# Gated attention in one core: seven block products for the Q projection, as a stage of its own

## The chip, the cores and the metric

The kernel runs on one core of one Trainium2 chip. A core has five engines that run side by side and wait for one another through semaphores: TensorE (matrix products; PE in the profile, and PEld for its weight loads), VectorE (DVE), ScalarE (ACT), GpSimd (POOL) and SyncE (SP), which here only issues transfers. TensorE writes to PSUM, eight banks of 128 x 512 float32; everything else lives in SBUF, and DRAM is reached by DMA. The metric is device time in microseconds. Two runs of the kernel before gave 1958.55 and 1958.67, a median of 1958.61.

## What is computed

The input x has 2048 tokens of 640 features. It is normalized per token, and the result feeds two branches that are multiplied at the end:

```python
def _A_ref(x, k_cache, v_cache, wq, wo):          # 32 heads of 128, last 512 keys of the cache
    q = (x @ wq) split into heads
    scores = einsum("bhqd,bhkd->bhqk", q, k) * DH**-0.5
    p = softmax(scores, axis=-1)
    o = einsum("bhqk,bhkd->bhqd", p, v)
    return o merged over heads @ wo
def _B_ref(x, w1, b1, w2, b2):                    # 640 -> 1728 -> 640
    h = relu(x @ w1 + b1) ** 2
    return h @ w2 + b2
xn = layernorm(x)
out = x + _A_ref(xn, ...) * silu(_B_ref(xn, ...))
```

All data are float32. A product of two float32 matrices is made of three TensorE products: each operand is split into a high part (what TensorE keeps of it) and a low remainder, and high x high, high x low and low x high are summed. So every product of a 128 x 128 block with a 128 x 512 block costs three matmuls of 512 columns, and every operand costs a copy (ScalarE) and a subtraction (VectorE or GpSimd) for its split.

## The kernel before

The tokens form four tiles of 512 (`NTILE`), the 640 features five chunks of 128 (`DC`), the 1728 hidden features of the MLP thirteen chunks and a half one (`FC`), the 512 keys four chunks (`KC`). Heads are worked in pairs (`G` = 2), token tiles in two halves of two.

The first 300 us normalize the tiles and run the MLP of three of the four tiles, with its split weights kept in SBUF; the MLP of the last tile is spread over the beginning and the end of the attention. The split x of each tile goes to DRAM (`xT_d`) and is read back when its half begins.

The attention is a list of 128 units, one for a head and a token tile. For unit i, TensorE forms the scores (`s_mm`, 12 matmuls into four PSUM banks of tag `s`), the value product of the unit before (`v_mm`, 12), the Q projection of the unit after the next (`q_mm`, 15 matmuls with x as the moving operand and wq as weights), and, per pair of units, the output products (`r_mm`, 30). VectorE folds each score bank by a transposing maximum (`max_fold`, tile rdm), ScalarE gathers the folded rows (`gather`), VectorE takes the row maximum (`row`, tile rowm), SyncE stores it to DRAM (m_d) and reads it back as a broadcast over the partitions (bm), and VectorE subtracts it (`shift`, tile e), which frees the score bank. ScalarE takes the exponential (`expo`) and the high part (`p_hi`, tile pt), GpSimd the low part (`p_lo`) and the sum of the halves (`s_add`). The row sums go the same way as the maxima, through s_d and bs, and scale the value product (`o_norm`).

The order is written out by hand: each step is put in a list with a time, `on(when, f, ...)`, relative to its unit's start in a grid of 12.4 us (`PERIOD`), and the list is sorted and issued. The times set the order on every engine's queue; they are not waited for. `load_raw` and `prep` bring and split the weights of the next heads. On SyncE's queue, `row` issues the small store and then the broadcast, which waits for the store to land. `align` puts NOPs between TensorE's instructions so that each unit is 128 of them and stands at the same place in blocks of 256.

Of the kernel before, what the change touches and what calls it, by code (L numbers as in the profile page):

```python
# [8 lines left out]
F32 = mybir.dt.float32  # L9
# [5 lines left out]
P = 128  # L15
# [3 lines left out]
BLOCK = 256  # L19
FIRST_SLOT = 188  # L20
SLOTS = (0, 11, 22, 33, 42)
LEAD_SLOT, LEAD_PADS, LEAD_STEPS = 76, 5, range(19, 23)
# [3 lines left out]
def kernel(  # L26
# [24 lines left out]
    LN_AT = {t: (3, 7) if t == LATE else (5, 9) for t in range(1, NTILE)}  # L51
    SCALE = DH**-0.5
    G = 2
    HALF = 2
    PSUM = bass.MemoryType.PSUM

    cpool = ctx.enter_context(tc.tile_pool(name="const", bufs=1))
    dpool = ctx.enter_context(tc.tile_pool(name="dram", bufs=1, space=bass.MemoryType.DRAM))

# [3 lines left out]
    b1_sb, b2_sb = b_sb[:, :FC], b_sb[:, FC : FC + DC]  # L63
    chunks = [(f0, min(P, F - f0)) for f0 in range(0, F, P)]
# [4 lines left out]
    class Ordered:  # L69
# [16 lines left out]
    xT_d = [  # L86
        [dpool.tile([P, DC, NT], F32, name=f"xT_d{t}_{i}") for i in range(2)]
        for t in range(NTILE)
    ]
    g_d = [dpool.tile([P, DC, NT], F32, name=f"g_d{t}") for t in range(LATE)]  # L90
    s_d = [dpool.tile([P, DC, NT], F32, name=f"s_d{t}") for t in range(NTILE // 2)]
    h_d = {f: dpool.tile([P, NT], F32, name=f"h_d{f}") for f in range(FC - 4, FC)}
# [4 lines left out]
    def products(ps, pairs, first=True, last=True):  # L97
        n = len(pairs)
        for i, ((ah, al), (bh, bl)) in enumerate(pairs):
            nc.tensor.matmul(ps, ah, bh, start=first and i == 0, stop=False)  # L100
            nc.tensor.matmul(ps, ah, bl, start=False, stop=False)  # L101
            nc.tensor.matmul(ps, al, bh, start=False, stop=last and i == n - 1)  # L102

    psx = ctx.enter_context(tc.tile_pool(name="psx", bufs=1, space=PSUM))

    FO, FA = FC - 3, FC - 4
    keep = ctx.enter_context(tc.tile_pool(name="keep", bufs=1))
    mctx, wctx, hctx = ExitStack(), ExitStack(), ExitStack()
    wpa = wctx.enter_context(tc.tile_pool(name="mwa", bufs=1, side="right"))
    wpb = mctx.enter_context(tc.tile_pool(name="mwb", bufs=1))  # L110
    xp = mctx.enter_context(tc.tile_pool(name="mx", bufs=2))
    hp = mctx.enter_context(tc.tile_pool(name="mh", bufs=2))
    ps_h = hctx.enter_context(tc.tile_pool(name="ps_h", bufs=2, space=PSUM, side="right"))
    ps_y = mctx.enter_context(tc.tile_pool(name="ps_y", bufs=DC, space=PSUM))

    w1s, w2s = [], []
    for f, (f0, n) in enumerate(chunks):
        wp = wpa if f < FO else wpb
        if n < P:
            w1s.append([wp.tile([P, DC, 2 * n], F32R, name=f"w1s{f}")])  # L120
        else:
            if f < FA:
                w1p = [wp.tile([P, DC, n], F32R, name=f"w1s{f}_{i}") for i in range(2)]
            else:
                two = keep.tile([P, 2, D], F32R, tag="ot", name=f"w1s{f}", bufs=4)
                w1p = [two[:, i, :].rearrange("p (c n) -> p c n", n=n) for i in range(2)]
            w1s.append(w1p)
        w2s.append([wp.tile([P, D], F32R, name=f"w2s{f}_{i}") for i in range(2)])

    def pad(pool, nbytes):  # L130
        pool.tile([P, nbytes // 4], F32, name="pad")

    pad(wpa, 480)

    def ln_tile(t, b):
        tag = "stage" if b < 2 else "mr"
        return xp.tile([P, D], F32, tag=tag, name=f"xb{t}_{b}")

    LS = {}

    def ln_load(t):
        mv = xp.tile([P, 4, NB], F32, tag="mv", name=f"mv{t}")[:, :2, :]
        sc = xp.tile([P, 3, NB], F32, tag="sc", name=f"sc{t}")
        xn = []
        for b in range(NB):
            xb = ln_tile(t, b)
            r0 = t * NT + b * P
            nc.sync.dma_start(xb, x[r0 : r0 + P, :])
            xn.append(xb)
        LS[t] = mv, sc, xn  # L150

    def ln_block(t, b):
        mv, sc, xn = LS[t]
        st = xp.tile([P, 2, 6], F32, tag="st", name=f"st{t}_{b}", bufs=4)
        hd = D // 2
        for i in range(2):
            dve.bn_stats(st[:, i, :], xn[b][:, i * hd : (i + 1) * hd])
        dve.bn_aggr(mv[:, :, b], st)

    def ln_var(t):  # L160
        mv, sc, xn = LS[t]
        dve.tensor_scalar(sc[:, 0, :], mv[:, 1, :], EPS, None, op0=ALU.add)
        nc.scalar.activation(sc[:, 1, :], sc[:, 0, :], AF.Sqrt)

    def ln_root(t):
        mv, sc, xn = LS.pop(t)
# [7 lines left out]
        return mv  # L174

    def ln_rows(t, mv):
        pm = psx.tile([P, NT], F32, tag="x", name=f"pmv{t}")
        nc.tensor.transpose(pm[: 2 * NB, :P], mv.rearrange("p a b -> p (a b)"), ident)
        row = xp.tile([2 * NB, P], F32, tag="lr", name=f"lr{t}", bufs=1)
        nc.vector.tensor_copy(row, pm[: 2 * NB, :P])  # L180
        d = dpool.tile([2, NT], F32, name=f"mv_d{t}")
        nc.sync.dma_start(d.rearrange("a (b p) -> (a b) p", p=P), row)
        bc = []
        for i in range(2):
            m = xp.tile([P, D], F32, tag="mr", name=f"mr{t}_{i}")[:, :NT]
            nc.sync.dma_start(m, d[i : i + 1, :].to_broadcast([P, NT]))
            bc.append(m)
        xs = [
            keep.tile([P, DC, NT], F32R, tag="acc", name=f"xT{t}_{i}", bufs=2)
            if t % 2  # L190
            else xp.tile([P, DC, NT], F32R, tag=f"xT{i}", name=f"xT{t}_{i}", bufs=1)
            for i in range(2)
        ]
        return bc, xs

    def ln_chunk(t, bc, xs, c):
        xc = xp.tile([P, D], F32, tag="stage", name=f"xc{t}_{c}")[:, :NT]
        nc.sync.dma_start(xc, xT[c * P : (c + 1) * P, t * NT : (t + 1) * NT])
        dve.tensor_tensor(xc, xc, bc[0], op=ALU.subtract)
        nc.vector.tensor_tensor(xc, xc, bc[1], op=ALU.mult)  # L200
        nc.scalar.activation(xs[0][:, c, :], xc, AF.Copy)
        nc.vector.tensor_tensor(xs[1][:, c, :], xc, raw(xs[0][:, c, :]), op=ALU.subtract)

    PRE, BOTH, BR = {}, {}, []

    def biases():
        pb = psx.tile([P, NT], F32, tag="x", name="pb")
        pe.transpose(pb[:, :P], BR.pop(), ident)
        dve.tensor_copy(b1_sb, pb[:, :FC])
        dve.tensor_copy(b2_sb, pb[:, 32 : 32 + DC])  # L210
        split_lo(0, PRE[0, 1], 1, dve)

    def first_reads(br):
        for k in range(2):
            load_part(0, k, k == 0)
# [6 lines left out]
        for f in (1, 2):  # L222
            for k in range(2):
                load_part(f, k)
        return [PRE[0, k] for k in range(2)]

    def ln_first():
        mv = xp.tile([P, 4, NB], F32, tag="mv", name="mv0")
        sc = xp.tile([P, 3, NB], F32, tag="sc", name="sc0")
# [1013 lines left out]
```

## Time and profile before

| | |
|---|---|
| median of two runs | 1958.61 us |
| span of the profiled execution (its own time beside the span isn't told) | 1956.9 us |
| TensorE busy | 1949.2 us, 8612 matmuls |
| VectorE, ScalarE, GpSimd busy | 1537.3, 1187.6, 1376.7 us |
| moved by DMA | 219.13 MB, mean 112 GB/s |
| TensorE clock granted | 1.0 in all but the last stretch |

The profile is one execution on the chip. Its page has the busy time by engine, the chain of work that ended last, and groups of equal instructions with their mean duration and what ended the idle time before them. From the trace come tables by stretch of time, the instructions in order of time, and for a tile how long its transfers took from issue to landing. A matmul's duration there includes its pipeline; the pitch of a row of matmuls is what counts.

### The profile page before, as it was taken

Reading aid. Unit: us, or ns where it says so; the run is one execution under the profiler, and the core shown is the slowest. Engines: PE = TensorE matmul, PEld = TensorE weight load, DVE = VectorE, ACT = ScalarE, POOL = GpSimd, SP = SyncE. Lnnn points to the kernel's source line nnn. Section 1 sums busy time; section 2 is a strip of 40 time slices with the busy share of each in tenths; the row PEclk is TensorE's granted clock in tenths of the full one; section 3 lists DMA queues with packets and bytes.
Section 4 is the critical chain, followed back from the end, with each engine's and each line's share of the span. In section 5 each row is a group of like instructions: output and inputs, shape, how many; then the busy total and the mean of one; then the engine's idle time right before and its main releaser. Section 6 shows DMA issues by size and latency. Waiting matters only on the chain.

```text
span 1956.9 us, 28182 instructions
## 1 busy us (share of the span) xinstructions
PE 1949.2 (100%) x8612; PEld 1612.5 (82%) x8612; DVE 1537.3 (79%) x2638; ACT 1187.6 (61%) x2040; POOL 1376.7 (70%) x757
## 2 busy tenths in 40 slices
PE   9999999999999999999999999999999999999998
PEld 7888888888888888888888888888888888888887
DVE  6523337788888888888888878888888888888865
ACT  5432336766666666666666676666666666666643
POOL 2121226888888888888888888888888888888841
PEclk9999999999999999999999999999999999999999
DMA  6330454333333332332335434433333333332353
GB/s 189 88 119 28 185 198 130 97 94 92 93 92 93 92 92 92 92 92 93 93 91 179 141 117 109 114 114 114 114 113 114 113 114 114 98 92 92 85 189 118
DMA packets 127892, 219.13 MB, mean 112 GB/s; under 512 B 23452, under 2 KB 38086, under 8 KB 126470
## 3 DMA queue, kind: packets, MB, share of 16 engines
q1 hardware_dynamic: 124742, 202.75, 34.3%
q0 software_dynamic: 2864, 14.42, 1.8%
q8 instruction: 77, 1.26, 0.2%
q14 instruction: 65, 0.53, 0.1%
q10 hardware_dynamic: 144, 0.16, 0.0%
HBM read 193.41 MB, written 23.87 MB: 111 GB/s over the span
## 4 chain that ended last, share of the span: by engine, by line
PE 99%; DVE 0%; DMA 0%; ACT 0%; issue 0%; POOL 0%; POOLq 0%
PE pq L77 22%; PE r L77 22%; PE o L77 18%; PE s L77 18%; PE ph L431 7%; PE ly L77 2%; PE py L101 2%; PE py L100 2%; PE py L102 2%; PE lu L77 2%; PE eu L77 1%; PE ph L398 0%; PE py L454 0%; PE py L453 0%; DMA xb<-in_x_dram 0%; PE px L77 0%
## 5 line engine op out<-in xcount | busy, mean ns | idle before, releaser
L77 POOL TENSOR_TENSOR pt<-e,pt 128x1024 fp32r<-128x1024 f32 x256 | 615.8, 2405 | 113.6 <-ACT pt L77 68.2
L77 PE MATMUL r<-ot,wo 128*128 128x512 f32 x1920 | 496.6, 389 | 0.0
L77 PE MATMUL pq<-ax,wq 128*128 128x512 f32 x1920 | 456.1, 389 | 0.0
L77 PEld LDWEIGHTS pq<-ax,wq 128*128 128x128 f32 x1920 | 360.4, 188 | 75.2 <-DVE q L77 0.4
L77 PEld LDWEIGHTS r<-ot,wo 128*128 128x128 f32 x1920 | 360.5, 188 | 74.8
L77 PE MATMUL o<-pt,wv 128*128 128x512 f32 x1536 | 369.2, 389 | 0.0
L77 PE MATMUL s<-q,wk 128*128 128x512 f32 x1536 | 369.0, 389 | 0.0
L77 DVE TRANSPOSE_TENSOR_REDUCE rdm<-s 128x16 f32<-128x512 f32 x512 | 347.6, 712 | 6.0 <-PE s L77 5.8
L77 ACT ACTIVATE e<-e 128x1024 f32<-128x1024 f32 x256 | 269.8, 1054 | 123.8 <-DVE e L77 80.5
L77 PEld LDWEIGHTS o<-pt,wv 128*128 128x128 f32 x1536 | 288.3, 188 | 60.1 <-POOL pt L77 0.4
L77 PEld LDWEIGHTS s<-q,wk 128*128 128x128 f32 x1536 | 288.4, 188 | 59.8
L77 DVE TENSOR_TENSOR e<-s,bm 128x512 f32<-128x512 f32 x512 | 312.3, 665 | 5.8 <-DMA bm<-m_d 5.4
L77 POOL TENSOR_TENSOR su<-e,e 128x1024 f32<-128x1024 f32 x128 | 309.2, 2415 | 0.0
L77 ACT ACTIVATE pt<-e 128x1024 fp32r<-128x1024 f32 x256 | 271.9, 1062 | 6.9
L77 DVE TENSOR_TENSOR acc<-r,acc 128x512 f32<-128x512 f32 x300 | 203.6, 679 | 12.7 <-PE r L77 12.4
L77 ACT ACTIVATE rdm<-rdm 32x64 f32<-32x64 f32 x384 | 97.7, 254 | 182.1 <-DVE rdm L77 179.0
L77 DVE TRANSPOSE_TENSOR_REDUCE rds<-su 128x32 f32<-128x1024 f32 x128 | 158.4, 1237 | 0.3 <-POOL su L77 0.3
L77 DVE TENSOR_TENSOR ot<-o,ot 128x512 fp32r<-128x512 f32 x128 | 88.5, 692 | 86.1 <-ACT ot L77 86.1
L77 ACT ACTIVATE q<-pq 128x512 fp32r<-128x512 f32 x128 | 76.7, 599 | 113.6 <-PE pq L77 113.6
L431 PE MATMUL ph<-xT,w1s 128*128 128x512 f32 x585 | 139.0, 389 | 0.0
L431 PEld LDWEIGHTS ph<-xT,w1s 128*128 128x128 f32 x585 | 109.7, 188 | 22.8
L77 ACT ACTIVATE rds<-rds 32x32 f32<-32x32 f32 x384 | 89.7, 234 | 60.1 <-DVE rds L77 56.6
(137 smaller groups left out, 1942.3 us busy)
## 6 DMA issues: line engine op xcount, KB each, us to landing
bm<-m_d SPq DMA_DIRECT2D x128, 256.0 KB, 3.2
bs<-s_d SPq DMA_DIRECT2D x128, 256.0 KB, 4.0
qr<-in_wq_dram SPq DMA_DIRECT2D x64, 320.0 KB, 4.5
or<-in_wo_dram SPq DMA_DIRECT2D x64, 320.0 KB, 4.7
kr<-in_kT_dram SPq DMA_DIRECT2D x64, 256.0 KB, 4.3
vr<-in_v_dram SPq DMA_DIRECT2D x64, 256.0 KB, 4.3
xT_d<-xT POOLq DMA_DIRECT2D x6, 1280.0 KB, 7.6
ax<-xT_d SPq DMA_DIRECT2D x4, 1280.0 KB, 11.3
```

The source lines that it names most:

```text
L77: ins = method(*args, **kwargs)
L100: nc.tensor.matmul(ps, ah, bh, start=first and i == 0, stop=False)
L101: nc.tensor.matmul(ps, ah, bl, start=False, stop=False)
L102: nc.tensor.matmul(ps, al, bh, start=False, stop=last and i == n - 1)
L431: nc.tensor.matmul(ph, w1s[f][i][:, c, :], xs[j][:, c, :], start=k == 0, stop=k == len(order) - 1,)
```

## The change

The MLP no longer stands first. The kernel now begins with the layer norm and the whole Q projection of all four token tiles, and writes each split Q (high and low, 512 KB for a head and a tile) to DRAM (`q_d`).

For ten heads of the first two tiles the projection is as before, 15 matmuls per head and tile (`conv_mm`). For the other 22 heads there, and all 32 heads of the last two tiles, two heads and two tiles are taken together. Four of the five feature chunks form a 2 x 2 block product, whose eight block products are replaced by seven on sums and differences of blocks (`WINO`, `s_sum`, `t_sum`), with four accumulating banks a to d and some sums made by ScalarE and VectorE in between; the fifth chunk is added as before. A group of two heads and two tiles takes 54 matmuls in place of 60. While this runs, the MLP's weights are split once and stored in DRAM (`pre_split`, `pre_store`).

Then come the 128 attention units. `q_load` reads Q from DRAM, behind bm on SyncE's queue. Score banks are allocated in pairs, and `max_fold` and `shift` work on two banks at once; `s_add` writes over e. Where the Q products stood, a planner (`spread`) puts pieces of the MLP, of all four tiles, so that each unit has about the same number of matmuls; the pieces' operands (x, h, weights) are read from DRAM, and h is stored there. The square of the MLP's ReLU moves from GpSimd to ScalarE. `align` and its NOPs are gone. The gate and the end of the last tiles are rearranged (`close_1`, `close_2`).

```diff
-    def q_mm(i, cs):
-        hf, g, t, h = units[i]
-        if 0 in cs:
-            QPS[i] = bank(f"pq{i}", 1)
-        ws, xs = WQ[hf, h], XT[hf, t]
-        for c in cs:
-            triple(QPS[i], ...)
+    WINO = (
+        ("a", (0, LOW), (0, LOW), True, True),
+        ("b", (0, HIGH), (0, HIGH), True, False),
+        ("b", (0, LAST), (0, LAST), False, True),
+        ("a", ("S", 2), ("T", 2), False, True),
+        ("c", ("S", 1), ("T", 1), True, True),
+        ("d", ("S", 4), (1, HIGH), True, False),
+        ("a", ("S", 3), ("T", 3), False, True),
+        ("d", (0, LAST), (1, LAST), False, True),
+        ("c", (1, LAST), (1, LAST), False, True),
+        ("a", (1, HIGH), ("T", 4), False, False),
+        ("a", (1, LAST), (0, LAST), False, True),
+    )
...
+    def q_store(key, h, t):
+        sp.dma_start(q_d[h, t], raw(QO.pop(key)))
+    def q_load(i):
+        hf, g, t, h = units[i]
+        q = pools["ep"].tile([P, 2, NT], F32R, tag="q", name=f"q{i}", bufs=AHEAD + 1)
+        sp.dma_start(raw(q), q_d[h, hf * TPH + t])
+        Q[i] = (q[:, 0, :], q[:, 1, :])
...
     def s_mm(i, c):
-        SC[i, c] = pools["psb"].tile([P, NT], F32, tag="s", name=f"s{i}_{c}", bufs=KC)
+        if c % 2 == 0:
+            SC[i, c // 2] = two_banks(f"s{i}_{c // 2}")
...
-    def max_fold(i, c):
+    def max_fold(i, k):
         dve.tensor_reduce(
-            RD[i, "m"][:, :, 0, c],
-            SC[i, c].rearrange("p (i b) -> p b i", i=B32),
+            RD[i, "m"][:, :, 0, 2 * k : 2 * k + 2].rearrange("p b c -> p c b"),
+            SC[i, k].rearrange("p c (i b) -> p c b i", i=B32),
...
-    def shift(i, c):
-        dve.tensor_tensor(E[i, k][:, half, :], SC.pop((i, c)), MB[i], op=ALU.subtract)
+    def shift(i, k):
+        m = MB[i][:, None, :].to_broadcast([P, 2, NT])
+        dve.tensor_tensor(E[i, k], SC.pop((i, k)), m, op=ALU.subtract)
...
+        on(-2 * PERIOD + 4.34 if i > 1 else -10.0 + i, q_load, i)
         for c in range(KC):
-            on(0.68 * c, align, i, SLOTS[c])
             on(0.68 * c, s_mm, i, c)
+            if c % 2:
+                on(0.8 + 0.68 * c, max_fold, i, c // 2)
+                on(10.0 + 0.4 * c, shift, i, c // 2)
         on(3.95, gather, i, "m")
         on(4.1, row, i, "m")
...
-        on(PERIOD + 4.0, p_hi, i, 1)
+        on(PERIOD + 1.5 + late, p_hi, i, 1)
...
-        on(2 * PERIOD + 4.2, o_norm, i)
+        on(2 * PERIOD + 4.0, o_norm, i)
...
+    target = 44.0
+    while True:
+        filler, rest = spread(target)
+        if not rest:
+            break
+        target += 0.25
```

1464 lines of the change are left out of this document (754 added, 710 removed).

## The prediction

> **What bounds the kernel now.** I read the page's busy line and chain first, then the windows, to see whether any stage is not TensorE's.
>
> ```profile
> span 1956.9 us, 28182 instructions
> ...
> PE 1949.2 (100%) x8612; PEld 1612.5 (82%) x8612; DVE 1537.3 (79%) x2638; ACT 1187.6 (61%) x2040; POOL 1376.7 (70%) x757
> ...
> PE 99%; DVE 0%; DMA 0%; ACT 0%; issue 0%; POOL 0%; POOLq 0%
> ```
>
> The chain that ended last is 99% matmuls: no other engine is waited for anywhere for long. The columns of the next rows are the stretch, its length, busy time and count by engine, granted clock, DMA share and GB/s.
>
> ```profile
> 0.00:20.00 20.00, 17.48 (x93) 15.00 (x94) 13.18 (x36) 12.72 (x22) 6.17 (x16) 1.00 0.80 255
> 700.00:1000.00 300.00, 300.00 (x1325) 248.50 (x1324) 264.53 (x455) 197.72 (x343) 244.72 (x124) 1.00 0.31 93
> 1900.00:1957.00 57.00, 51.78 (x229) 42.56 (x227) 29.34 (x38) 21.73 (x33) 11.51 (x8) 0.98 0.44 140
> ```
>
> In the middle TensorE is busy without a gap at full clock: 300.00 / 1325 = 0.226 us a matmul. The idle 7.7 us (1956.9 - 1949.2) lies in the lead and the tail. So the time is the number of matmuls times their pitch, as long as nothing makes TensorE wait. The question is what the change does to both factors. For the second I need one attention unit in order of time (start, length, engine).
>
> ```profile
> 1007.27 2.88 PE L77 MATMUL s<-q,wk 128*128 128x512 f32 x12
> 1008.15 2.76 DVE L77 TRANSPOSE_TENSOR_REDUCE rdm<-s 128x16 f32<-128x512 f32 x4
> 1010.94 0.79 ACT L77 ACTIVATE rdm<-rdm 32x64 f32<-32x64 f32 x3 [1.67 <-DVE rdm L77]
> 1011.76 0.41 DVE L77 TENSOR_REDUCE rowm<-rdm 32x16 f32<-32x256 f32 x1 [0.85 <-ACT rdm L77]
> 1012.20 0.33 SPq L77 DMA_DIRECT2D m_d<-rowm  x1
> 1013.57 0.33 SPq L77 DMA_DIRECT2D bm<-m_d  x1
> 1017.40 2.43 DVE L77 TENSOR_TENSOR e<-s,bm 128x512 f32<-128x512 f32 x4
> 1019.51 2.88 PE L77 MATMUL s<-q,wk 128*128 128x512 f32 x12
> ```
>
> From scores to scores the unit takes 1019.51 - 1007.27 = 12.24 us, 54 matmuls at 0.2267. Under it runs a round trip: scores, four folds, gather, row maximum, a small store (m_d), its broadcast back (bm), the subtraction (e) that frees the score banks, the next scores. It has room here: the first e ends near 1018.0, the scores that need its bank start at 1019.51.
>
> **The change part by part.** *Matmuls.* Before, the Q products are 1920 matmuls of 512 columns. After, 20 products of 15 (ten heads, two token tiles) and 27 groups of 54 instead of 60: 300 + 1458 = 1758. Scores (1536), values (1536), output (1920) and MLP (1640) keep their counts. So 162 go: 162 x 0.2267 = **36.7 us**, and with nothing else the span would be 1920.2. (The Trainium skill, "TensorE: Matmul & The Clock Gate", the section on the 56 ns gap, gives 215.7 ns for back-to-back matmuls of 512 columns; by that the gain would be 34.9 us. The trace has 226.7, and it decides.)
>
> *The attention unit.* Scores 12, values 12, output 15 on average, and MLP pieces filled in by a planner whose target ends at 51.25 matmuls: 51.25 x 0.2267 = **11.62 us** in place of 12.24. The round trip must now fit in 11.62, and the change lengthens it. Durations (mean ns after the busy us):
>
> ```profile
> L77 DVE TRANSPOSE_TENSOR_REDUCE rdm<-s 128x16 f32<-128x512 f32 x512 | 347.6, 712 | 6.0 <-PE s L77 5.8
> L77 DVE TRANSPOSE_TENSOR_REDUCE rds<-su 128x32 f32<-128x1024 f32 x128 | 158.4, 1237 | 0.3 <-POOL su L77 0.3
> L77 DVE TENSOR_TENSOR e<-s,bm 128x512 f32<-128x512 f32 x512 | 312.3, 665 | 5.8 <-DMA bm<-m_d 5.4
> L77 DVE TENSOR_TENSOR acc<-r,acc 128x512 f32<-128x512 f32 x300 | 203.6, 679 | 12.7 <-PE r L77 12.4
> L77 PEld LDWEIGHTS s<-q,wk 128*128 128x128 f32 x1536 | 288.4, 188 | 59.8
> L77 DVE SCALAR_TENSOR_TENSOR q<-pq,q 128x512 fp32r<-128x512 f32 x128 | 83.7, 654 | 4.3 <-ACT q L77 4.3
> L77 ACT ACTIVATE q<-pq 128x512 fp32r<-128x512 f32 x128 | 76.7, 599 | 113.6 <-PE pq L77 113.6
> L77 POOL TENSOR_TENSOR wq<-qr,wq 128x640 fp32r<-128x640 f32 x62 | 98.0, 1580 | 28.8 <-ACT wq L77 28.1 <-PE o L77 0.7
> ```
>
> Folds and subtractions now take two banks at once. A fold of 1024 costs 1.237 (the rds row) where 512 cost 0.712, so the last fold ends 0.525 later; before, it too waited for the last score bank. Scores to bm issue: 1013.57 - 1007.27 + 0.525 = 6.83. The subtraction of 1024 is not in the trace; between 0.665 and 2 x 0.665, by the fold's step 0.665 + 0.525 = 1.19, and only its end frees the pair of banks. Then TensorE must load weights (0.188) before the first matmul: 0.25 with the hand-off. The round trip is 6.83 + L + 1.19 + 0.25 = **8.27 + L**, L being bm from issue to landing. Everything hangs on L. The rows below are from bm over the whole run, bm in 1095 to 1150 (stores of accumulators behind it), bm in 1026 to 1080 (loads of xT behind it) and bs, then the queue around one bm and one bs.
>
> ```profile
> DMA to landing us min/median/max: 3.0/3.2/3.9
> DMA to landing us min/median/max: 3.4/3.5/3.6
> DMA to landing us min/median/max: 3.8/3.8/3.8
> DMA to landing us min/median/max: 3.5/4.0/4.7
> ...
> 1050.43 0.32 SPq L77 DMA_DIRECT2D bm<-m_d  x1
> 1050.79 0.43 SPq L77 DMA_DIRECT2D ax<-xT_d  x1
> ...
> 1018.81 0.32 SPq L77 DMA_DIRECT2D bs<-s_d  x1
> 1019.17 0.43 SPq L77 DMA_DIRECT2D or<-in_wo_dram  x1
> 1019.72 0.38 SPq L77 DMA_DIRECT2D kr<-in_kT_dram  x1
> ```
>
> bm and bs are the same broadcast of 256 KB. Alone it lands in 3.2; with a transfer or two issued 0.4 us behind it, 3.5 to 4.0. Before, almost nothing follows bm. After, by the order of the queue, `q_load` (512 KB) follows 126 of the 128, and in 77 of these a weight, x or h tile or a store of 256 to 640 KB besides. I take L = 3.65, between the two windows in which something does follow a bm; the ends are 3.2 and 4.0. The round trip is then 11.92 against 11.62, and TensorE waits 0.30 us before the scores of 127 units: **+38 us**.
>
> *The other engines in that stage* have room, so I cost them at nothing. VectorE: 264.53 / 300 x 12.24 = 10.8 us a unit, less q (0.654), less 0.37 and 0.28 from the paired folds and subtractions, plus 0.5 for MLP pieces at 0.7 each: 10.0 of 11.6. ScalarE stays near 8.1, GpSimd loses half a wq (0.79) and has 9.2. Where one was late, TensorE would wait by that much. One place is close: the output product of chunk 2 needs the accumulation of chunk 1, which VectorE does after the row maximum; it is due at about 6.1 us after the scores, and the product is reached at 27 x 0.2267 = 6.1.
>
> *The first stage* has 1758 x 0.2267 = 399 us of matmuls behind the same lead. Its helpers (copies of 0.6, sums of 0.7) have waits of their own on TensorE, since three of the products accumulate in one bank that ScalarE must copy in between; the shortest of these gaps is 6 matmuls, 1.36 us. More doubtful is the queue: 67.1 MB of Q, 24.2 of wq, 10.5 of split x, 27.4 of MLP weights and 10.6 for the layer norm are 140 MB in 410 us, 341 GB/s.
>
> ```profile
> DMA packets 127892, 219.13 MB, mean 112 GB/s; under 512 B 23452, under 2 KB 38086, under 8 KB 126470
> 274.00:284.00 10.00, 10.00 (x45) 8.26 (x45) 2.44 (x4) 2.47 (x4) 1.10 (x2) 1.00 0.97 365
> 113.00:119.00 6.00, 6.00 (x28) 4.99 (x27) 0.79 (x2) 0.81 (x2) 2.62 (x4) 1.00 0.97 341
> ```
>
> A nearly full queue moved 341 to 365 GB/s. So the transfers need 383 to 410 us: just enough, with four Q buffers to lag behind. Between no loss and some 35 us (a backlog that the buffers don't take up) I put **+6 us**. Lead, tail and the dropped `addr_align` I put at zero: no row shows what a block crossing costs.
>
> *Sum:* 1956.9 - 36.7 + 38 + 6 = 1964; the median of the two runs, 1958.61, stands 1.7 above the span, so **1966 us**, 0.4% slower, which is no change by the 2% that a measurement of this kernel can tell.
>
> **The rivals.**
>
> *A, TensorE stays the bound.* bm is ahead of q in the queue, and if what follows doesn't touch it, L is 3.2, the round trip 11.47 is under 11.62, and the stage runs at TensorE's pace: 1956.9 - 36.7 + 6 + 1.7 = 1928. For it: bm's median over the run, and the round trip's own room before. Against: every row with something behind the broadcast is above 3.2. With no loss in the first stage either it is 1922, the best that the matmul count allows.
>
> *B, slower.* Place: bm in each unit. Price: L = 4.0, as bs with two loads behind it, gives 12.27 a unit, 127 x 0.65 = 83 us: 2011. The change breaks even at L = 3.59 (36.7 - 6 over 127 units is 0.24) and is 2% slower from L = 3.90. For it: q alone is as many bytes as two of the loads behind bs. Against: it is one transfer, and the windows with one have 3.4 to 3.8.
>
> *C, the first stage doesn't bring its gain.* The seven products wait for their copies, or for a full queue, by 1 us in each of 27 groups and 10 us in the products before: 31 us more than in A, 1959, with the attention stage at its pace.
>
> *D, memory under load.* The attention stage would move some 355 MB in 1500 us (Q 67, MLP weights 72, h 59, bm and bs 67, K, V and output weights 55, the rest 35), 237 GB/s where the row above has 93. If that lifted every bm to the longest landing of such a broadcast in the trace, 4.7, the trip would be 12.97 and the time 1928 + 127 x 1.35 = 2099. For it: the traffic is 2.5 times what it was. Against: 4.7 is a maximum, not a median. The Trainium skill states a rule of this kind ("DMA: Bandwidth & Descriptors", Latency and other measured facts): a memory access takes 0.2 us on average and 2 us at high load. By its figures L would be 3.2 + 1.8 = 5.0 and the time, as an estimate, near 2137; of those 1.8 us the trace bears out 0.8, bs at 4.0 beside its loads.
>
> **How the numbers follow.** Forecast (1945 to 1990): 0.42. A (1920 to 1945): 0.28. B (1990 to 2030): 0.17. C (around 1959, other cause): 0.10. D: 0.03. The range leaves out D, the upper part of B and the edge of A: 1922 to 2013. Faster by over 2% needs less than 1919.4, below the floor of 1922 unless lead or tail shrink: 0.04. Slower by over 2%, above 1997.8, is most of B, D and the forecast's upper edge: 0.21. The rest, 0.75, is within 2%.
>
> **What would show it.** In the profile of the changed kernel: PE x8450 matmuls, at 0.2267 where they are packed; units of 11.9 us with idle time before `s`, released by VectorE's e, which itself waits for bm; bm landing in about 3.65; DMA share above 0.6 in the attention stage and above 0.9 in the first. If units are 11.62 and bm is 3.2, A holds. If the first stage takes over 410 us from the lead, C. I am wrong altogether if TensorE waits on something not in the round trip, such as bs ahead of the row maximum, or GpSimd's second half of the split probabilities.

## The result and the profile after

The changed kernel takes **2471.86 us** (two runs, 2471.83 and 2471.9) against 1958.61: 1.262 times the time before, with an interval of 1.2584 to 1.2657. The forecast was 1966, the range 1922 to 2013. The profiled execution took 2471.9 with a span of 2469.6, so 505.6 us more than the 1964 of the prediction's sum have to be found.

From the page of the changed kernel, the busy line and the chain that ended last by engine and by line:

```profile
PE 2093.0 (85%) x8450; PEld 1625.1 (66%) x8450; DVE 1730.6 (70%) x2443; ACT 1297.9 (53%) x2287; POOL 1411.6 (57%) x768
...
DMA 33%; PE 30%; DVE 15%; issue 10%; ACT 6%; POOL 4%; SPq 1%; DVEq 0%; ACTq 0%; POOLq 0%
DMA s_d<-rows 12%; DMA bs<-s_d 8%; PE s L79 7%; PE r L79 6%; PE o L79 4%; PE pw_a L79 4%; DMA bm<-m_d 3%; PE mu L79 3%; DMA wr<-in_wq_dram 2%; DMA m_d<-rowm 2%; PE md L79 2%; DVE rds L79 2%; DVE acc L79 2%; POOL pt L79 2%; SPq L79 1%
```

The matmuls are as many as counted, 8450. But the chain, 99% matmuls before, is now led by transfers, and by two that the prediction's round trip did not contain: the 2 KB store of the row sums, s_d, and its broadcast bs. The transfers of the loop, with the median from issue to landing in us, after:

```profile
bm<-m_d SPq DMA_DIRECT2D x128, 256.0 KB, 4.4
bs<-s_d SPq DMA_DIRECT2D x128, 256.0 KB, 4.0
...
m_d<-rowm SPq DMA_DIRECT2D x128, 2.0 KB, 1.9
s_d<-rows SPq DMA_DIRECT2D x128, 2.0 KB, 4.7
```

Before, bm and bs had 3.2 and 4.0, and the two small stores

```profile
m_d<-rowm SPq DMA_DIRECT2D x128, 2.0 KB, 1.3
s_d<-rows SPq DMA_DIRECT2D x128, 2.0 KB, 1.3
```

**A store of 2 KB now takes 4.7 us in place of 1.3.**

Where the time lies is seen from the windows, cut at the first scores, at the scores of units 16 and 127, and at the end (length, busy and count by engine, clock, DMA share, GB/s):

```profile
0.00:468.70 468.70, 422.62 (x1770) 334.48 (x1771) 379.13 (x607) 231.66 (x454) 196.26 (x164) 0.96 0.85 303
468.70:732.70 264.00, 210.18 (x830) 161.85 (x828) 161.51 (x212) 146.26 (x255) 142.61 (x70) 0.92 0.53 177
732.70:2391.90 1659.20, 1413.32 (x5690) 1093.67 (x5691) 1158.40 (x1580) 903.50 (x1554) 1033.39 (x508) 0.96 0.55 179
2391.90:2469.60 77.70, 46.92 (x162) 35.10 (x162) 31.53 (x47) 16.49 (x26) 39.36 (x26) 0.85 0.38 121
```

Length minus count times 0.2267 is what each stretch loses. Before, the same four cuts lost -1, 0, 0 and 5 us (below zero since 60 short transposes are counted as matmuls).

| stretch | lost after | lost before | predicted increase | above the prediction |
|---|---|---|---|---|
| to the first scores | 67 | -1 | 6 | 62 |
| units 0 to 15 | 76 | 0 | 5 | 71 |
| units 16 to 126 | 369 | 0 | 33 | 336 |
| from the last scores | 41 | 5 | 0 | 36 |

Two thirds lie in the steady attention, where a unit takes 14.98 us in the mean, not 11.92. Two units in order of time (in brackets, idle time before a row and what ended it; "issue" where the profile shows nothing that was waited for):

```profile
1202.98 0.70 DVE L79 TENSOR_TENSOR o<-o,bs 128x512 f32<-128x512 f32 x1 [0.40 <-DMA bs<-s_d]
1203.59 0.40 DVE L79 TENSOR_REDUCE rowm<-rdm 32x16 f32<-32x256 f32 x1
...
1204.01 0.33 SPq L79 DMA_DIRECT2D m_d<-rowm  x1
...
1206.25 0.33 SPq L79 DMA_DIRECT2D bm<-m_d  x1
...
1206.62 0.42 SPq L79 DMA_DIRECT2D q<-q_d  x1
1207.10 0.90 SPq L79 DMA_DIRECT2D h_d<-hs  x2
...
1208.05 0.47 SPq L79 DMA_DIRECT2D mh<-h_d  x1
...
1208.63 0.92 SPq L79 DMA_DIRECT2D s_d<-rows  x1
...
1212.44 4.22 PE L79 MATMUL s<-q,wk 128*128 128x512 f32 x12 [2.07 <-issue]
...
1215.06 0.32 SPq L79 DMA_DIRECT2D bs<-s_d  x1
...
1218.54 0.70 DVE L79 TENSOR_TENSOR o<-o,bs 128x512 f32<-128x512 f32 x1 [0.58 <-DMA bs<-s_d]
```

Follow s_d. It is issued at 1208.63, behind bm, q, two stores of h and a load of h, some 1.8 MB; bs, which waits only for it, goes out at 1215.06, so the 2 KB took 6.4 us. bs lands near 1218.5; `o_norm` waits for it, and since it now stands ahead of the row maximum on VectorE, the row maximum, m_d, bm and the next scores wait too. Behind the row maximum, VectorE does an accumulation, the low half of the value product (ot) and the fold of the next row sums (rds), from which the next s_d comes, at 1223.49. That one has only bm and q ahead of it and takes 2.8 us. So there is a second loop beside the prediction's: s_d, bs, `o_norm`, the work on the row sums, s_d. The chain of waits in the same stretch runs along it (start, length, what):

```profile
1191.68 6.28 DMA s_d<-rows
1197.98 4.98 DMA bs<-s_d
...
1205.18 1.16 DVE rds L79
...
1208.63 6.42 DMA s_d<-rows
1215.06 3.45 DMA bs<-s_d
...
1220.74 1.16 DVE rds L79
...
1223.49 2.79 DMA s_d<-rows
...
1251.64 3.83 issue
1255.47 5.46 PE s L79 x12
...
1271.02 3.01 PE s L79 x12
```

The prediction's loop stays closed as well. In 84 of the 109 units from 17 to 125 TensorE waits more than 0.3 us before the scores, 167 us in all; each time the scores start about 0.1 us behind the end of the `e` that frees their banks, while q had landed 12.7 us before them or earlier. So it is `e`, and not a late q, that the scores wait for.

I took the 109 stores s_d between 750 and 2380 us from the trace and set each one's time against the bytes issued before it and not yet landed (a transfer under way counted by the part of its time that is left): up to 200 KB 1.3 to 1.6 us (3 stores); 200 to 500 KB, median 2.6 (26); 500 to 800 KB, 4.2 (34); 800 to 1200 KB, 5.4 (31); above, 6.5 (15). The line through them is **1.5 us plus 0.98 us for every 256 KB outstanding**, 267 GB/s, with a correlation of 0.97; for m_d it is 1.2 plus 1.24, also 0.97.

### The profile page after: what moved, and what is told of

Its sections match the earlier page's. It is cut to its first block, busy times and chain, and to the rows that moved or that the text cites. A ratio compares the mean times of both kernels' runs of the same rounds, so it can differ in the third digit from the quotient of the medians.

```text
span 2469.6 us, 26821 instructions
## 1 busy us (share of the span) xinstructions
PE 2093.0 (85%) x8450; PEld 1625.1 (66%) x8450; DVE 1730.6 (70%) x2443; ACT 1297.9 (53%) x2287; POOL 1411.6 (57%) x768
## 4 chain that ended last, share of the span: by engine, by line
DMA 33%; PE 30%; DVE 15%; issue 10%; ACT 6%; POOL 4%; SPq 1%; DVEq 0%; ACTq 0%; POOLq 0%
DMA s_d<-rows 12%; DMA bs<-s_d 8%; PE s L79 7%; PE r L79 6%; PE o L79 4%; PE pw_a L79 4%; DMA bm<-m_d 3%; PE mu L79 3%; DMA wr<-in_wq_dram 2%; DMA m_d<-rowm 2%; PE md L79 2%; DVE rds L79 2%; DVE acc L79 2%; POOL pt L79 2%; SPq L79 1%
## 5 line engine op out<-in xcount | busy, mean ns | idle before, releaser
L79 DVE TENSOR_TENSOR e<-s,bm 128x1024 f32<-128x1024 f32 x256 | 301.4, 1218 | 247.5 <-DMA bm<-m_d 246.5
L79 DVE TRANSPOSE_TENSOR_REDUCE rdm<-s 128x32 f32<-128x1024 f32 x256 | 319.5, 1250 | 103.6 <-PE s L79 89.5
L79 POOL TENSOR_TENSOR e<-e,e 128x1024 f32<-128x1024 f32 x128 | 306.4, 2394 | 10.0
L79 PE MATMUL md<-mh,md 128*128 128x512 f32 x820 | 213.3, 402 | 17.9 <-DVE y L79 8.8
L79 PE MATMUL mu<-mx,mu 128*128 128x512 f32 (+1 forms) x820 | 209.5, 398 | 10.5 <-ACT pt L79 4.0
L79 PEld LDWEIGHTS md<-mh,md 128*128 128x128 f32 x820 | 157.9, 193 | 57.0 <-DVE y L79 9.7
L79 PEld LDWEIGHTS mu<-mx,mu 128*128 128x128 f32 (+1 forms) x820 | 154.8, 189 | 50.1 <-ACT pt L79 4.6
L79 POOL TENSOR_TENSOR wv<-vr,wv 128x512 fp32r<-128x512 f32 x64 | 83.8, 1310 | 163.7 <-ACT wv L79 128.7
L79 DVE TENSOR_TENSOR o<-o,bs 128x512 f32<-128x512 f32 x128 | 88.1, 688 | 123.7 <-DMA bs<-s_d 123.4
L79 DVE TRANSPOSE_TENSOR_REDUCE rds<-e 128x32 f32<-128x1024 f32 x128 | 157.6, 1231 | 14.3 <-POOL e L79 13.7
```

The lines of the kernel that those rows point to most:

```text
L79: ins = method(*args, **kwargs)
```

## The experiments

Times of the kernel before beside these runs lay between 1958.35 and 1959.18. The table has one run of each; the four columns in the middle are means over units 16 to 125, worked out from the issue and landing times in the trace.

| run | us | unit | m_d | bm | s_d | first scores at |
|---|---|---|---|---|---|---|
| before | 1958.6 | 12.24 | 1.43 | 3.21 | 1.37 | 298 |
| changed | 2471.9 | 14.98 | 2.25 | 4.27 | 4.44 | 468.7 |
| e1, no bulk | 2163.9 | 12.61 | 1.34 | 3.18 | 1.37 | 465.4 |
| e6a, q alone | 2203.5 | 12.90 | 1.36 | 3.86 | 2.16 | 468.9 |
| e6b, MLP alone | 2312.7 | 13.69 | 2.04 | 3.71 | 2.75 | 466.8 |
| e13, before with 1.5 MB | 2311.3 | 15.04 | 3.60 | 4.34 | 5.29 | 298 |
| e18, before with 0.5 MB | 1998.8 | 12.56 | 1.68 | 3.99 | 2.12 | 300 |
| e19, before, 1.5 MB behind bs | 2215.2 | 14.30 | 4.07 | 3.26 | 2.38 | 298 |
| e2, `o_norm` behind | 2471.2 | 14.91 | 2.84 | 4.38 | 4.07 | 467.3 |
| e15, one bank | 2477.5 | 15.03 | 2.31 | 4.37 | 4.58 | 467.8 |
| e3, small stores on ScalarE | 2450.7 | 14.82 | 2.17 | 4.37 | 4.17 | 468.9 |
| e4, q and h on ScalarE | 2498.6 | 15.16 | 3.49 | 3.82 | 3.82 | 467.6 |
| e5, bulk behind bs | 2436.4 | 14.57 | 3.30 | 3.26 | 2.20 | 466.1 |
| e10, before, 51 matmuls | 1921.5 | 11.95 | 1.61 | 3.20 | 1.39 | 298 |
| e8, no bulk, r early | 2331.7 | 13.99 | 1.33 | 3.21 | 1.47 | 469.4 |
| e11, behind bs, r early | 2598.1 | 15.90 | 2.62 | 3.27 | 2.06 | 465.8 |
| e14, no bulk, one bank | 2152.9 | 12.49 | 1.37 | 3.25 | 1.44 | 468.0 |
| e7, late norm | 2495.8 | 15.14 | 2.23 | 4.31 | 4.51 | 468.7 |
| e12, no bulk, late norm, no split | 2159.0 | 12.65 | 1.36 | 3.25 | 1.37 | 456.1 |
| e16, late Q stores | 2497.4 | 15.19 | 2.23 | 4.38 | 4.54 | 462.5 |

### Is it the traffic?

**e1: the bulk transfers left out.** The tiles stay, their loads are issued once.

```diff
     def q_load(i):
+        if i > AHEAD:
+            Q[i] = Q[i - AHEAD - 1]
+            return
...
     def big(kind, t, k):
+        if n in KEPT:
+            MBIG[kind, t, k] = KEPT[n]
+            return
...
     def up_store(t, f):
-        for i in range(2):
-            sp.dma_start(h_d[t, f][:, i, :], ...)
```

> The changed kernel with the same instructions on the engines, but the bulk transfers of the attention stage are left out: q, the MLP's x, h and weight tiles are loaded once into the buffers that the kernel has for them and used again, and the h stores are dropped (so Q and the MLP are computed from wrong operands). Theory 1 (the 2 KB stores m_d and s_d and the broadcasts bm and bs land late behind the bulk transfers, and bs then holds up the row maximum, since o_norm now stands ahead of it on VectorE): m_d falls from 2.25 to 1.4 us, s_d from 4.4 to 1.5, bm from 4.3 to 3.3, the mean unit from 15.0 to 11.7 to 12.0, the time from 2472 to between 2080 and 2130, as the first stage keeps its losses. Theory 2 (the new order, the two-bank tiles and the MLP pieces make the unit long whatever the transfers do): units stay above 13.5 and the time above 2290.

2163.9 us: 308 go. The transfers of this run:

```profile
bm<-m_d SPq DMA_DIRECT2D x128, 256.0 KB, 3.2
bs<-s_d SPq DMA_DIRECT2D x128, 256.0 KB, 3.7
...
m_d<-rowm SPq DMA_DIRECT2D x128, 2.0 KB, 1.3
s_d<-rows SPq DMA_DIRECT2D x128, 2.0 KB, 1.3
```

All four land as early as in the kernel before or earlier, with every instruction of the engines in place. Theory 1 holds for the transfers; its 2130 was too low, since a unit is still 12.61 against 11.62 of matmuls.

**e13: the other way round, only the traffic added to the kernel before**, as copies from DRAM to DRAM.

```diff
         bc = ap.tile([P, NT], F32, tag=f"b{what}", name=f"b{what}{i}", bufs=2)
         sp.dma_start(bc, d.rearrange("a b -> (a b)")[None, :].to_broadcast([P, NT]))
+        for n in range(2 if what == "m" else 1):
+            far = dpool.tile([2, P, W], F32, name=f"far{what}{i}_{n}")
+            sp.dma_start(far, kT[2 * (i % 16) : 2 * (i % 16) + 2])
```

> The kernel before with about the changed kernel's traffic added and nothing else: in each unit two copies of 512 KB from DRAM to DRAM directly behind bm and one directly behind bs, 1.5 MB that nothing uses. Theory 4 (a small transfer waits for what was issued ahead of it and hasn't landed; it costs only where the round trip has no room): bm rises from 3.2 to 4.7, s_d, issued 3.9 us behind bm, to 2.2, m_d stays near 1.4; the trip of 4.95 + 1.4 + 4.7 and 1.0 to the next scores still fits into 12.24, so 1960 to 1995. Theory 11 (this much traffic costs by itself, whatever the order): units above 13.5, the time above 2120.

2311.3: 353 us slower, units of 15.04. Its small stores:

```profile
m_d<-rowm SPq DMA_DIRECT2D x128, 2.0 KB, 3.3
s_d<-rows SPq DMA_DIRECT2D x128, 2.0 KB, 5.0
```

Theory 11 has the time; I had left m_d at 1.4, and it rose to 3.6. So the kernel before with about this traffic has a unit as long as the changed one: the seven products and the pieces as such aren't needed to explain it. The mean traffic here is 186 GB/s and a DMA share of 0.59 (700 to 1000 us); in the mean, neither is full.

**e6a and e6b: which traffic.** e6a is e1 with q loaded again, without the first edit above; e6b is the changed kernel with that first edit alone.

> The run without bulk transfers, with the loads of q put back behind bm; the MLP's x, h and weight tiles are still loaded once only and h isn't stored (so the MLP is computed from wrong operands). Theory 4: 512 KB behind bm have nearly gone when s_d is issued 2.7 us later, so s_d 1.3 to 2.0, bm 3.7, m_d 1.35; units 0.1 to 0.4 longer than the 12.61 without bulk, the time 2175 to 2215. If the 64 MB of Q are what the change pays for, units above 13.5 and the time above 2280.

> The changed kernel with the loads of q left out (three tiles of Q are loaded once and used by all units, so the scores are wrong); the MLP's transfers stay. Theory 4: they bring most of the loss, about 1.2 MB a unit beside K, V and output weights: s_d 3 to 3.8 us, m_d about 2, bm 4.2, units 13.6 to 14.4, the time 2300 to 2400. If Q's transfers are what counts, units below 13.0 and the time below 2230.

2203.5 and 2312.7, both as theory 4 had them in time (in e6b s_d, 2.75, and bm, 3.71, stayed below what it had). Q adds 40 us to e1, the MLP 149, both together 308, more than the sum of 189. s_d goes with this: it gains 0.8, 1.4 and 3.1 over e1. Why the two cost more together than apart was not tested.

**e18 and e19: dose and place.** The edit of e13 with one copy behind bm and none behind bs, and with three behind bs and none behind bm.

> The kernel before with one copy of 512 KB from DRAM to DRAM behind each bm and nothing else: a third of the traffic that took its units to 15.04 us, as many bytes as q has. Theory 4 (a small transfer waits for what is outstanding, and the round trip has some 1.3 us of room): bm 3.7, s_d 1.6 to 2.4 as it is issued 3.9 us later, m_d 1.4 to 1.8, and the trip 4.95 + 1.6 + 3.7 + 1.0 still fits: units of 12.24 to 12.4, 1958 to 1985. Theory 11 (traffic costs in proportion to its bytes): a third of 353 us, 2075.

> The kernel before with three copies of 512 KB behind each bs and none behind bm: the bytes of the run with 1.5 MB a unit, in another place. Theory 4 (the place decides what is outstanding when a small transfer is issued): s_d back to 1.4 and bm to 3.3, but some 2.1 MB behind bs take 8 us and reach the next m_d, 3.5 in place of 1.4; units of 12.6 to 13.3, 2010 to 2095. Theory 11 (the bytes decide): units of 15 again, 2310.

Both came out between the theories. A third of the bytes costs 40 us, not 118: there is some room, and what is left grows faster than the bytes. The same 1.5 MB in another place cost 257 in place of 353: s_d falls from 5.29 to 2.38, and m_d rises from 3.60 to 4.07, as the bytes now stand ahead of it. The place matters, the bytes more.

### Through which order?

**e2: `o_norm` put back behind the row maximum.** `on(2 * PERIOD + 4.0, o_norm, i)` becomes 4.2, `o_hi` 4.22.

> The changed kernel with o_norm (which waits for bs) put back behind the row maximum on VectorE, as in the kernel before; nothing else. Theory 1 (late transfers, coupled through o_norm): the row maximum no longer waits for bs, scores to m_d falls from 6.77 to 5.5 us, m_d and bm stay at 2.25 and 4.3, so the mean unit goes from 15.0 to 13.7 and the time to about 2310. Theory 3 (the order of these two alone is the cause): units go back to 12.0 and the time to about 2100. If the late bs then stalls VectorE just behind the row maximum and takes back what was won, units stay above 14.5.

Nothing changes: 2471.2. Scores to m_d falls from 6.77 to 6.01, but m_d rises to 2.84: it leaves earlier and lands hardly earlier. What I had called the cause of 1.30 us a unit is only where the wait was seen. The edit doesn't open the second loop either: `o_norm` still stands on VectorE ahead of the fold of the row sums, from which the next s_d comes.

**e15: score tiles of one bank**, four folds and four subtractions, as before.

```diff
-            if c % 2:
-                on(0.8 + 0.68 * c, max_fold, i, c // 2)
-                on(10.0 + 0.4 * c, shift, i, c // 2)
+            on(0.8 + 0.68 * c, max_fold, i, c)
+            on(10.0 + 0.4 * c, shift, i, c)
```

> The changed kernel with all its transfers and score tiles of one bank, nothing else. If the round trip sets the unit as the sum 6.77 + 2.25 + 4.27 + 1.67 of the changed kernel says, it shortens by 0.5 ahead of m_d and 0.5 behind bm: units of 14.0, 2345. If the late row sums hold the unit (s_d 4.4 and bs 4.1, with o_norm ahead of the row maximum), what is won is waited for there: units above 14.6, the time above 2420.

2477.5. The shortest way from scores to m_d is indeed 0.5 shorter (4.93 against 5.47), the mean is 7.06 against 6.77: what was won is waited for. So the row maximum's trip alone does not set the unit. The chain of this run, from 800 to 1800 us, is s_d for 22%, bs 15%, m_d 9% and bm 8%: it runs along both loops.

**e3 and e4: another queue.** e3 issues m_d, s_d and mv_d by ScalarE (`act.dma_start(d, r)`), e4 the loads of q and the stores of h.

> The changed kernel with the small stores alone (m_d, s_d of 2 KB, and mv_d of 4 KB in the layer norm) issued by ScalarE, on a queue that nothing else uses; bm, bs and all bulk transfers stay on SyncE's queue. Theory 1a (a small store is late because it stands behind bulk transfers in its own queue): m_d 1.4 us and s_d 1.5 to 2 in place of 2.25 and 4.4, bs is in time, scores to m_d 5.5, bm still 4.3, so units of 12.7 and a time near 2180, with 10 to 20 us of it from the first stage. Theory 1b (it is late because the memory or the DMA engines are busy, whatever the queue): the stores stay above 2 and 4 us, units above 14.3, the time above 2400.

> The changed kernel with the loads of q and the stores of h (77 of the roughly 300 KB to 2 MB of bulk a unit) issued by ScalarE on a queue of their own, so that they no longer stand between m_d, bm and s_d on SyncE's queue. Theory 1a (order in the queue): s_d falls from 4.4 us to below 3, m_d below 2, bm to 3.8 or less, units to 13.0 or less, the time below 2250. Theory 1b (the DMA engines and the memory are shared whatever the queue): s_d stays near 4, bm at 4.3, and the time within 60 us of 2472, plus what ScalarE loses to issuing, 0.4 us for each of two transfers a unit.

The small stores on a queue of their own:

```profile
m_d<-rowm ACTq DMA_DIRECT2D x128, 2.0 KB, 1.4
s_d<-rows ACTq DMA_DIRECT2D x128, 2.0 KB, 4.6
```

1b in both. s_d still takes 4.6 in the median with nothing ahead of it in its queue (m_d gains 0.5 in the median and 0.08 in the mean), and e4, which takes 0.7 MB a unit (q 0.5, h 0.2) off SyncE's queue, is not faster either: s_d and bm both fall to 3.82, but m_d rises to 3.49. The Trainium skill ("DMA: Bandwidth & Descriptors", Queues, rings and completion order) says that a transfer's semaphore write lands only after every earlier write of the same DMA engine, across its queues. The two runs agree with that; they don't show the mechanism itself.

**e5: the bulk loads behind bs only** (the stores of h stay where they were), by `SPOTS = (8.9,)` for loads and q_load at 8.85 in place of 4.34.

> The changed kernel with q and the MLP's x, h and weight loads all issued behind bs; of the bulk only h stores still follow bm. Nothing is left out. Rows so far: s_d and m_d take 1.3 to 1.5 us plus about 1 us for every 256 KB that was issued before them and has not landed, on whichever queue. Theory 4 (a small transfer waits until what is outstanding has gone, so the place of the bulk decides): s_d falls to about 2 us; the bulk behind bs, some 2.3 MB with K, V and output weights, drains in 8.5 to 9.3 us and runs into the next m_d, which rises to 3.5; bm 3.3, scores to m_d 5.5, so units of 13.6 and a time near 2300. Theory 5 (the bytes decide, not the place): units stay at 14.7 to 15.2, the time at 2440 to 2500.

2436.4: 35 us, where theory 4 had 170. s_d falls to 2.20 and bm to 3.26 as it said, and m_d rises to 3.30; but the unit is 14.57, not 13.6, and that is nearer to theory 5. As in e19, the bytes move to the next small store.

### What else is in a unit?

**e10: the kernel before with 51 matmuls a unit** (`if c == DC - 1: continue` in `q_mm`).

> The kernel before with the last of the five feature chunks left out of every Q product (so Q is wrong): 12 matmuls in place of 15, 51 a unit in place of 54, as many as a unit of the changed kernel has; everything else as it was. If matmuls are paid at their pitch and the rest of a unit fits into 51 of them, 384 x 0.2267 = 87 us go: 1872 us, units of 11.56. If another part of the unit is already too long for that (its round trip is 4.95 + 1.43 + 3.21 us and the e that follows, VectorE has 10.2 us of work), units stay above 11.8 and the time above 1900.

1921.5: 37 us gained of 87. TensorE's weight loads wait here, in units 16 to 126, for

```profile
PEld o L77 <- POOL pt L77: 54.3, 107, 1.2
```

(us in total, times, the longest): GpSimd's low half of the probabilities, 107 times in 111 units. So the arrangement that the change starts from can't run 51 matmuls at their pitch: a unit is 11.95, not 11.56. This was there before the change, hidden by three matmuls.

**e14: e1 with score tiles of one bank.**

> The run without bulk transfers, with score tiles of one bank, four folds and four subtractions of 512, as in the kernel before (VectorE gets 0.65 us more work a unit). If the 1.0 us by which a unit of that run is longer than its 51.25 matmuls comes from the two-bank tiles (folds end 0.5 later, banks come free 0.5 later), units fall from 12.61 to 12.0 and the time from 2164 to 2090. If it comes from the one bank r, whose next product waits for an accumulation behind the row maximum, and from GpSimd's second half of the split probabilities, units stay at 12.4 or more and the time above 2140.

2152.9, 11 us less: the two-bank tiles are not what makes most of e1's unit 1.0 too long. In e1 TensorE waited, from 694 to 2092 us, for

```profile
PE r L79 <- DVE acc L79: 31.6, 31, 2.9
PE s L79 <- DVE e L79: 14.7, 11, 2.3
PE o L79 <- POOL pt L79: 13.0, 19, 1.4
```

and half of this is the one bank r. The kernel before had two, which it shared with the Q products.

**e8 and e11: an edit for that wait.** The product of chunk 1 goes ahead of the next scores: `R_AT` (3, 2.75) becomes (2, 12.35); e8 without bulk, e11 with it and with e5's order.

> The run without bulk transfers (one load of each q, x, h and weight buffer, no h stores), with the output product of chunk 1 moved on TensorE from behind the next scores to just ahead of them, so that its accumulation is no longer done behind the row maximum while TensorE waits for the one bank r. Theory 9 (what is left above 51.25 matmuls in that run, 1.0 us a unit, is mostly this wait): units fall from 12.61 to 11.9 to 12.1, the time from 2164 to 2090 to 2110. Theory 10 (it is something else: the two-bank subtraction or the split probabilities, and the wait only moves to the scores): units stay at 12.4 or more, the time above 2140.

> The changed kernel, nothing left out, with two edits together: q and the MLP's loads behind bs only, and the output product of chunk 1 ahead of the next scores. If the late transfers set the unit, the wait for the bank r lies mostly beside them, and the second edit adds little to the 2436 of the first alone: 2395 to 2440. If both add, 2370.

Misses: 2331.7 and 2598.1, 168 and 162 slower than without the edit. Between 800 and 2000 us the wait of `r` for acc rose from 29.4 to

```profile
PE r L79 <- DVE acc L79: 96.5, 41, 3.0
```

since the accumulation of chunk 0 stands on VectorE behind the subtractions, which wait for bm (in e8 the subtractions start at 1020.82, the accumulation at 1023.09, and `r` at 1023.83 after 2.37 us of waiting). These 67 us are a little over half of what e8's units lose there (1.38 us each, 119 in this stretch). The edit shows that my place for the product was worse; how e1's last microsecond divides is open beyond the rows above.

### The first stage

TensorE loses 43 of its 67 us between 100 and 200 us (252 matmuls), at a DMA share of 0.63, while later the transfers are full. The changed kernel, and e7 below it:

```profile
100.00:200.00 100.00, 70.78 (x252) 53.06 (x253) 85.39 (x134) 41.14 (x81) 23.52 (x14) 0.83 0.63 224
...
300.00:400.00 100.00, 97.54 (x422) 78.28 (x421) 83.93 (x132) 56.22 (x113) 50.56 (x44) 1.00 1.00 365
```

```profile
100.00:200.00 100.00, 78.10 (x302) 60.48 (x301) 82.07 (x136) 39.92 (x82) 22.16 (x14) 0.90 0.64 230
...
300.00:400.00 100.00, 93.65 (x397) 74.58 (x396) 80.54 (x125) 53.01 (x107) 51.34 (x47) 0.98 0.98 360
```

**e7** gives the layer norm of the last two tiles 16 us more; **e12** is e1 with that and with 2 of the 26 weight splits; **e16** has the stores of Q 2 us later in the written order (`q_store` at +4.4 for +2.4).

> The changed kernel with the layer norm of the last two token tiles given more time: between the row store mv_d with its broadcasts mr and the first subtraction stand 16 us more in the written order, and what depends on it (sums of tiles, stores of split x, the start of the MLP's weight splitting) is moved back by 12 to 28 us. Theory 6 (in the first stage too a small store and its broadcast land late behind bulk, and VectorE and ScalarE, working in order, hold up the copies that TensorE's block products wait for): the 28 us lost between 100 and 200 us fall below 10, the first scores come 20 to 30 us earlier than 468.7, the time is 2440 to 2455, the attention unit unchanged at 15.0. Theory 7 (the first stage is bound by its bytes, 140 MB): the stall only moves, the first scores stay within 8 us of 468.7.

> The run without bulk transfers, with the later layer norm of the run that gave it 16 us more, and without all but two of the 26 loads, splits and stores of the MLP's weights in the first stage (27 MB; the MLP uses two tiles for all). Theory 7 (the first stage's second half is bound by its bytes, so what a better order wins at 100 to 200 us is lost again at 200 to 470 us): with these bytes gone the gain stays, the first scores come at 440 to 455 in place of 465 to 469. If they stay above 462, the loss of the first stage is neither the order of the layer norm nor the bytes of the weights.

> The changed kernel with the stores of Q 2 us later in the written order of the first stage, so that fewer loads on SyncE's queue stand behind a store that still waits for its low half on VectorE. SyncE waited 43.5 us for that between 80 and 200 us. Theory 12 (the loss of 43 us at 100 to 200 us comes from this queue: loads of x for the layer norm issued late, their row stores and broadcasts later still): that wait falls below 25, the first scores come at 445 to 460 in place of 468.7, the time 2450 to 2465. If it is only the time that mv_d and mr take to land (3.8 to 6.5 and 5.9 us), the first scores stay above 464.

e7 won 50 matmuls between 100 and 200 us and had lost them all by the first scores, at 468.7 again: theory 7. Without the weights' bytes the first scores come at 456.1 (e12), 9.3 earlier than in e1 and 1 later than expected. e16 shortened SyncE's wait for the low halves of Q, between 80 and 200 us, from

```profile
SPq L79 <- DVE qo L79: 43.5, 16, 10.5
```

to 35.0 (expected below 25) and the first scores came 6 us earlier, between the two theories. So the order of the Q stores and the bytes both have a part; e12 still loses 55 of the 67 us, and for these no cause is shown. In e7 and e16 the steady unit rose to 15.14 and 15.19, where nothing was edited; I have no cause for that, so time differences of some 25 us between variants of the changed kernel are not read here, and e5's 35 stand little above that.

## Why the prediction was wrong

*Matmuls.* The count is right. That each is worth its pitch is wrong already for the kernel before: e10 got 0.097 us for each of 384 (37.3 / 384), because GpSimd, named as "wrong altogether if", stands just behind TensorE there. In the changed kernel the same weight loads wait 13.3 us for it in units 16 to 126, against 54.3; its floor of 1920 was out of reach for the other reasons below, since e1 has 2164 without the bulk.

*The attention unit: the failed step.* The form, scores to scores through m_d and bm, was right, and so were its instructions:

```profile
L79 DVE TENSOR_TENSOR e<-s,bm 128x1024 f32<-128x1024 f32 x256 | 301.4, 1218 | 247.5 <-DMA bm<-m_d 246.5
L79 DVE TRANSPOSE_TENSOR_REDUCE rdm<-s 128x32 f32<-128x1024 f32 x256 | 319.5, 1250 | 103.6 <-PE s L79 89.5
...
L79 DVE TENSOR_TENSOR o<-o,bs 128x512 f32<-128x512 f32 x128 | 88.1, 688 | 123.7 <-DMA bs<-s_d 123.4
```

(1.19 and 1.237 had been taken). But "everything hangs on L" made one transfer of four the variable:

| mean, us | predicted | after | e1 |
|---|---|---|---|
| scores to m_d | 5.46 | 6.77 | 5.61 |
| m_d | 1.37 | 2.25 | 1.34 |
| bm (L) | 3.65 | 4.27 | 3.18 |
| bm's landing to next scores | 1.44 | 1.67 | 2.47 |
| unit | 11.92 | 14.98 | 12.61 |

L was 0.6 too low, which alone is B's price and more. m_d was held at its quiet time, +0.9. Of the third, +1.3, the row maximum behind a late bs is 0.8: it starts 0.77 us behind its last gather, in e1 0.04. bs is late because s_d takes 4.44; the prediction named this wait at its end and gave it no price. With the row maximum ahead (e2) the 0.8 goes and m_d takes 0.6 more, so the price is that of the late s_d, not of the order. The rows that I used showed bm and bs beside one or two other transfers. None showed a 2 KB store behind 1 to 2 MB, and I took its quiet time without saying so: it was an operation that the trace of before did not show under that load (no m_d or s_d there has more than 200 KB outstanding at its issue, and the longest takes 2.5 us), and it should have been bounded. Of the 336 us that this stretch stands above the prediction, 262 go with the bulk (369 lost against 108 in e1). The other 75 are the 1.0 us of e1's unit less the 0.3 foreseen.

*Other engines at nothing.* Wrong by those 75 us, as far as the rows go. The close place was one: `r` waits 31.6 us for acc in units 16 to 126 of e1, and 75.8 in the changed kernel. The 27 matmuls before the product of chunk 2 hold only where the planner puts a piece of 9 in between. It also cuts pieces of 3; then `r` comes after 21, 4.8 us, against an accumulation at 6.1. In e1, in order of time, behind scores that began at 865.2:

```profile
867.95 1.55 PE L79 MATMUL r<-ot,wo 128*128 128x512 f32 x6
...
869.34 0.85 PE L79 MATMUL md<-mx,mu 128*128 128x512 f32 x3
...
871.31 1.66 PE L79 MATMUL r<-ot,wo 128*128 128x512 f32 x6 [1.12 <-DVE acc L79]
```

*First stage.* +6 was taken, at most 35; it is 68. The bytes were right (303 GB/s over 468.7 us are 142 MB against 140) and the full rate too (365 GB/s from 300 to 400 us), but the sum let them flow from the first microsecond, while 100 to 200 us ran at 224 GB/s with engines waiting in order. The DMA shares that were to show the forecast, above 0.6 in the attention and 0.9 in this stage, came out at 0.55 and 0.85, as the same bytes took longer.

*Lead and tail at zero.* The tail lost 36 more than before. There VectorE waits for

```profile
DVE o L79 <- DMA bs<-s_d: 16.5, 2, 10.7
```

and e1 still has 33 of its 41, so most of it is not the bulk that e1 leaves out. Units 0 to 15, in which the last block products and the first units overlap, are 71 above; half (35) goes with the bulk, the rest was not tried. No run put the NOPs of `align` back, so their part in any of this is not known.

*Rivals.* D, memory under load, was the one that happened, at a chance of 0.03, and it too priced bm alone. Three of the four transfers pay for the load: m_d 0.8, bm 1.1 and s_d 3.1 us more than before in the mean, s_d up to 7.9 in all; bs, 4.06 before, is 4.10. The Trainium skill's rule cited there gave L = 5.0 and 2137; L was 4.27 in the mean and at most 5.3. That size holds for the worst bm, and it is far too small for the 2 KB store.

*Break-even.* No run of mine brought the changed kernel near the time before. Even without bulk it is 2164.

## What to carry to other kernels

If a unit's loop goes through DRAM (a small store, then its broadcast), price each transfer on it under the traffic that will stand beside it, the 2 KB ones first. Here a small store took its quiet time plus about 1 us for each 256 KB outstanding at its issue, on ScalarE's queue as on SyncE's. The broadcast goes out when that store has landed and nothing of the bulk is outstanding, and pays for what follows it: bm took 4.3 in place of 3.2 us with about 1 MB issued in the 3 us behind it. A mean DMA share of 0.55 does not show this. And a bound that hides others by 2% (here TensorE over GpSimd and the round trip) gives only part of what is taken from it; the waits of the next engine tell how much, as 51 matmuls in the kernel before did for an edit of a few lines.

## What the runs showed of the hardware

That a 2 KB store is held up by bulk on other queues was not expected: 4.6 us on a queue of its own against 4.7.

A wait of TensorE costs more than its length. In the chain above, 3.83 us of waiting are followed by 12 score matmuls in 5.46 us, 0.455 each, twice the pitch; the ones at 1271.02 took 3.01. Over the changed kernel from 700 us on, the 12 matmuls after an idle time of 0.3 to 2 us had a median pitch of 0.24 (107 cases with no further gap in the 12), after 2 to 3.5 us 0.34 (25 cases), after 3.5 us and more 0.38 (20 cases). The granted clock goes with this. It was 1.0 ahead of all these waits, and 0.5 for a part of the 12 matmuls behind 2 of 58 waits of 1 to 2 us, 10 of 20 of 2 to 2.6 us, 5 of 5 of 2.6 to 3.5 us and 20 of 20 that were longer. Units 16 to 126 lost 246 us in idle time (1659.20 - 1413.32) and 123 in matmuls above their pitch (1413.32 - 5690 x 0.2267), at a granted clock of 0.96. The Trainium skill ("TensorE: Matmul & The Clock Gate", Part 1) has the array at half rate after an idle window of about 3.4 us. The trace agrees on the half rate and on the long waits, and shows it after many waits of 2 to 3.5 us too. The prediction had no such term, since its waits were 0.3 us.
